# Router inputs as 32 long rows turned by the matrix engine, v loads moved ahead of later q and k, a third v buffer, routing constants on GpSimd, and a new order

## The chip, the cores and the metric

The kernel runs on one core of one Trainium2 chip. The metric is device time in microseconds of one launch. TensorE is called PE here, VectorE DVE, ScalarE ACT, GpSimd POOL and SyncE SP; PEld is PE's loading of weights, which the profile lists apart.

## What is computed

Chunked attention with 4 x 8 heads of 768 positions and 64 columns: each chunk of 32 queries sees 8 memory keys and up to 56 keys around it. Its output, 3072 tokens of 512 columns, goes through a router with noise, and each token through the best two of eight two-layer experts.

```python
def _attn_ref(q, k, v, mem_k, mem_v):            # q, k, v: (4, 8, 768, 64), mem_*: (4, 8, 8, 64)
    chunk, left_ctx, right_ctx = (32, 16, 8)
    for c in range(nc):
        k_full = np.concatenate([mem_k, k[:, :, l_start:r_end]], axis=2)
        v_full = np.concatenate([mem_v, v[:, :, l_start:r_end]], axis=2)
        scores = scale * np.matmul(q_c, k_full.transpose(0, 1, 3, 2))
        a = softmax(scores)
        out[:, :, c_start:c_end] = np.matmul(a, v_full)

def _moe_ref(x, w_gate, w_noise, noise, w1, w2): # x: (3072, 512), noise: (3072, 8), w_gate, w_noise: (512, 8)
    logits = x @ w_gate + np.log1p(np.exp(x @ w_noise)) * noise
    top2, top2_w = best two of the 8 logits, and their softmax
    for e in range(8):                           # w1: (8, 512, 1024), w2: (8, 1024, 512)
        for k in range(2):
            mask = top2[:, k] == e
            out[mask] += top2_w[mask, k, None] * (np.maximum(x[mask] @ w1[e], 0.0) @ w2[e])
```

## The kernel before

All work is recorded as operations with a label (`op("lq", ...)`), each with an engine or a choice of engines (`DA` means DVE or ACT), an assumed duration, the operations it depends on, the buffers it takes or uses, and a priority. A planner in Python runs through these once, before the program is built: on each engine it takes the operation that can start first, and among near ties the one of lowest priority number. The table `SHIFT` adds a number to the priority of every operation of a label. The instructions are then written in the order of the planned starts, so every engine executes a fixed row of instructions; what they really wait for is settled by semaphores at run time. POOL's row holds most DMA issues, SP's row the rest.

**Attention.** Sixteen pairs of heads, two pairs to a group. For each group POOL issues one load of q (`lq`, L468), one of k (`lk`), and two of v (`lv`, L479, two or three DMAs). v goes into a tile `vg` of which there are two (`NV`); a tile comes free when both pairs of its group have been through `pvo`. For each pair: `tq` and `tk` turn q and k on PE (L509), `eq` and `ek` copy them out of PSUM (DVE or ACT, L355 and L357 are the two engines' copy lines), `sc` makes the scores (L532, L539), `mx` and `sb` take the largest and subtract it on DVE (L546, L562), `ex` is the exponential on ACT (L565), `tp`/`ep` turn the result, `pvo` multiplies by v (L584, L587), `rc` and `ml` normalise on DVE (L592, L605), and `tx`/`exx` turn the 128 columns for the router. There is one score buffer `ps_s` and one output buffer `ps_o`.

**Routing.** After every four pairs one batch of 768 tokens is complete. Its router runs as `lg` (logits, PE), `r1` (ACT), then on DVE `r2` (L665 to L680, the choice of two), `r3s`, `r4`, `r7` (gates, L861 to L865), `r6` and `r8a` (place in a list, L727 to L744), `r8` (`ohv`, L702), with `r3` (ranks, L693) and `r9` (the table of row numbers, L751) on PE. Labels end in `_s` for the third batch and `_l` for the last. `row_write` (L871) puts the rows of a batch, with their gates, into the DRAM table `x_rows`. The router needs the noise `nz_all`, the weights `wgn` and constants (`c_small`, L396 to L415).

**Experts.** Tokens are grouped by the pair of experts they chose: 28 lists of 128. The first two experts are "sealed": half of each of their lists is filled from the first three batches, so POOL gathers those rows (L907) when the third router is done, PE turns them (L938, copied to `XS`), and the first layers of both (`fo_a`, L1013) run before the last batch is routed. The other half follows after the last router. Then second layers (`so`, L1054), scaling and adding on DVE (L1065, L1073), and a scatter of each finished list by POOL (L1085). Each gather but the first few of the last batch is followed by a filler `rest` (L910) on POOL. w1 has three buffers, w2 four, the gathered rows `xl` eight (`NXL`).

Of the kernel before, what the change touches and what calls it, by code (L numbers as in the profile page):

```python
# [24 lines left out]
    "c_ones": 54.3, "c_small": -12.1, "c_wg": -35.9, "c_wgl": 7.9, "eq": 52.4, "ex": 1.2, "fo_a": 31.9, "gather": 41.0, "gather_a": 21.0,  # L25
# [5 lines left out]
    "so": 22.7, "sscat": -0.4, "stab": 7.4, "stab_s": 0.6, "sum": -4.1, "t_mk": 15.4, "tab": -3.8, "tab2": 15.6, "tab_l": -11.6, "take_o":  # L31
    -1.7, "tq": -14.7, "tt": -28.0, "tt_a": -40.9, "w_row": -52.7, "xev": 8.3, "xev_a": -32.5, "yo": 8.0, "z_k": 24.3, "z_row": -41.4,
    "z_v": -3.3}
# [26 lines left out]
class Planner:  # L60


    def __init__(self):
        self.ops, self.slots, self.held = [], {}, {}
        self.late, self.made, self.taken = [], {}, {}
# [15 lines left out]
    def op(self, label, engs, fn, deps=(), alloc=(), use=(), prio=0.0, dma=None, tag="", pace=0.0, mm=0, after=()):  # L81
        if isinstance(engs, tuple):
            engs = [engs]
        o = Op(engs, fn, list(deps) + list(after), list(alloc), list(use), prio + SHIFT.get(label, 0.0), dma, tag)
        o.label = label
        o.pace, o.mm, o.after = pace, mm, set(after)
# [16 lines left out]
    def run(self):  # L103
        free, dma_free, sync_free, lanes, paced, products, busy = {}, 0.0, 0.0, [], 0.0, 0, 0.0
        ready = [o for o in self.ops if o.wait == 0]
        attn_left = sum(o.tag == "attn" for o in self.ops)
        attn_end = 0.0
        order = []
        while ready:
            cand = {}  # L110
            for o in ready:
# [12 lines left out]
                for eng, dur in o.engs:  # L124
                    est = max(free.get(eng, 0.0), at)
                    if o.pace and attn_left:
                        est = max(est, paced)
# [36 lines left out]
            else:  # L164
                o.done = o.end + 0.12
# [18 lines left out]
            if o.tag == "attn":  # L184
                attn_left -= 1
                attn_end = max(attn_end, o.done)
                if attn_left == 0:
                    for s in self.late:
                        s.at = attn_end
# [6 lines left out]
def kernel(  # L196
# [39 lines left out]
    NGE, NQ, NV = 2, 2, 2  # L236
    NXL, NXR, NW1, NW2, NACC = 8, 3, 1, 3, 20
# [44 lines left out]
    fill(pl.pool("w2", 1), early, [128, FB, Dm], BF16, "w2t")  # L282
# [36 lines left out]
    neg = const.tile([128, left_ctx], BF16, name="neg")  # L319
    ramp_i = const.tile([128, 128], I32, name="ramp_i")  # L320
# [14 lines left out]
    wgn_f = rp.tile([128, PB, 2, E], F32, name="wgn_f")  # L335
# [25 lines left out]

    def ident_fn(o):
        make_identity(nc, identb)

    c_ident = op("ident", ("POOL", 0.6), ident_fn, prio=-98.5)
    z_v = []
    for i, s in enumerate(v_slots):
        z_v.append([op("z_v", ("DVE", 1.35), lambda o, s=s, j=j: V.memset(s.tile[:, j], 0.0), prio=(-85 + 0.1 * j) if i == 0 else -60 + i + 0.1 * j) for j in range(2)])  # L368
    c_ident32 = op("c_ident32", ("DVE", 0.2), lambda o: (V.tensor_copy(ident, identb[:32, :32]), V.tensor_scalar(out=minus, in0=identb, scalar1=-1.0, scalar2=None, op0=Alu.mult)), deps=[c_ident], prio=-79)
    c_ones = op("c_ones", ("DVE", 0.1), lambda o: (V.memset(onesb, 1.0), V.memset(neg, NEG)), prio=-86)  # L370
# [24 lines left out]
    def small_fn(o):  # L395
        V.memset(smin, 0.0)  # L396
        V.memset(flip, 0.0)
        for p in flipped:
            V.memset(flip[:, col(*p):col(*p) + 1], float(SL))
        for e in range(NSEAL):  # L400
            for p in row_of(e):
                V.memset(smin[:, col(*p):col(*p) + 1], float(SL))
# [822 lines left out]
```

## Time and profile before

| | |
|---|---|
| median of 3 runs | 334.55 us (332.03 to 334.84) |
| the profiled execution | 331.19 us, of which the span of its instructions is 329.6 us |
| PE busy | 282.8 us, 86% of the span |
| DVE, ACT, POOL busy | 161.9, 141.0 and 127.4 us |
| bytes moved by DMA | 42.75 MB |

A row of a timeline reads: start, busy time, engine and line, operation, output from inputs, shapes, and in brackets how long the engine stood idle before it and what ended that. A row of stretches reads: from and to, length, busy time of PE, PEld, DVE, ACT and POOL with the instruction count, the clock that PE was granted, the busy share of the DMA engines (above 1 where transfers overlap) and GB/s written. Times within the profile count from the start of the span.

### The profile page before, as it was taken

How to read it: one execution, taken by the hardware profiler on the slowest of the kernel's cores; microseconds unless marked ns; L12 is line 12 of the kernel's file. 1: busy time of each engine (PE TensorE's matmuls, PEld its weight loads, DVE VectorE, ACT ScalarE, POOL GpSimd, SP SyncE). 2: the span in 40 equal slices, each digit the busy share in tenths (PEclk: the TensorE clock that was granted, in tenths of full speed). 3: DMA queues.
4: the chain of work that ended last, by engine and by line, in shares of the span. 5: the costliest groups of instructions: out<-in, count | busy, mean ns of one | idle time of the engine just before them, and what ended most of it. 6: DMA issues, size and time to landing. Idle time of an engine off the chain costs nothing.

```text
span 329.6 us, 7497 instructions
## 1 busy us (share of the span) xinstructions
PE 282.8 (86%) x3090; PEld 178.0 (54%) x3090; DVE 161.9 (49%) x404; ACT 141.0 (43%) x265; POOL 127.4 (39%) x148
## 2 busy tenths in 40 slices
PE   1678767587676799799999999999999999999991
PEld 0567655475566567455647645444544744744540
DVE  6877997879889676254253043052042051041050
ACT  1468665656484265741504604604604604505500
POOL 8293353413504915898735221041040051051072
PEclk9999797979785569999999999999999999999997
DMA  9999999999993592939999995395390020021032
GB/s 99 202 157 148 180 148 176 193 133 204 145 166 114 152 153 59 182 98 195 191 215 220 255 196 74 55 207 74 57 203 28 3 113 23 2 111 50 3 121 83
DMA packets 83065, 42.75 MB, mean 130 GB/s; under 512 B 57017, under 2 KB 76474, under 8 KB 83026
## 3 DMA queue, kind: packets, MB, share of 16 engines
q0 software_dynamic: 74672, 38.78, 87.3%
q1 hardware_dynamic: 8066, 3.38, 4.2%
q8 instruction: 25, 0.41, 0.5%
q14 instruction: 14, 0.11, 0.2%
q10 hardware_dynamic: 288, 0.07, 0.1%
HBM read 61.26 MB, written 10.85 MB: 219 GB/s over the span
## 4 chain that ended last, share of the span: by engine, by line
PE 50%; DMA 12%; POOL 12%; issue 11%; DVE 10%; ACT 2%; POOLq 1%; DVEq 0%
PE ps_l L1013 16%; PE ps_l L1054 15%; DMA vg<-in_v_dram 9%; PE ps_g L1054 6%; PE ps_g L1013 5%; POOL xl L907 4%; DMA w2l<-in_moe_w_dram 3%; POOL out_dram L1085 2%; POOL rest L910 2%; POOL vg L479 2%; DVE vg L368 2%; DVE xrow L605 2%; PE ps_o L587 1%; PE ps_g L614 1%; ACT kT L355 1%
## 5 line engine op out<-in xcount | busy, mean ns | idle before, releaser
L1023 ACT ACTIVATE ht<-ps_l 128x384 bf16<-128x384 f32 (+2 forms) x123 | 54.8, 470 | 94.5 <-PE ps_l L1013 93.0
L1054 PEld LDWEIGHTS <-ht 128*128 128x128 bf16 x448 | 43.7, 98 | 52.2 <-DMA w2l<-in_moe_w_dram 0.6
L1013 PE MATMUL ps_l<-XS,w1t 128*128 128x384 bf16 (+4 forms) x416 | 61.0, 302 | 2.8 <-ACT XS L355 2.8
L1013 PEld LDWEIGHTS <-w1t 128*128 128x128 bf16 x544 | 43.9, 99 | 33.4 <-issue 4.3
L1085 POOL DMA_INDIRECT out_dram<-acc,oid x28 | 28.8, 1027 | 70.2 <-DVE acc L1073 66.4
L1054 PE MATMUL ps_l<-w2l,ht 128*128 128x512 bf16 x240 | 53.4, 379 | 0.3 <-DMA w2l<-in_moe_w_dram 0.3
L479 POOL DMA_DIRECT2D vg<-in_v_dram x18 | 23.6, 1314 | 34.7 <-PE ps_o L587 30.6
L1073 DVE SCALAR_TENSOR_TENSOR acc<-ps_l,gates,acc 128x512 f32<-128x512 f32 x17 | 12.8, 751 | 45.6 <-PE ps_l L1054 43.6
L1073 DVE SCALAR_TENSOR_TENSOR acc<-ps_g,gates,acc 128x512 f32<-128x512 f32 x11 | 8.3, 751 | 37.4 <-PE ps_g L1054 37.4
L355 ACT COPY kT<-ps_q 64x768 bf16<-64x768 bf16 x27 | 21.4, 792 | 11.7 <-PE ps_q L509 10.2
L1065 DVE TENSOR_SCALAR acc<-ps_l,gates 128x512 f32<-128x512 f32 x20 | 15.0, 751 | 19.0 <-PE ps_l L1054 18.8
L1054 PE MATMUL ps_g<-w2l,ht 128*128 128x512 bf16 x96 | 21.7, 379 | 0.0
L907 POOL DMA_INDIRECT xl<-x_rows,gid x16 | 16.8, 1049 | 11.6 <-PE ps_l L1054 4.0
L1013 PEld LDWEIGHTS <-w1l 128*128 128x128 bf16 x192 | 17.2, 98 | 7.0
L1013 PE MATMUL ps_l<-XS,w1l 128*128 128x256 bf16 (+3 forms) x152 | 20.5, 289 | 0.0
L509 PE MATMUL ps_q<-identb,qn 128*64 128x128 bf16 x192 | 10.7, 256 | 10.8 <-DMA qn<-in_q_dram 7.3
L1023 ACT ACTIVATE ht<-ps_g 128x384 bf16<-128x384 f32 (+2 forms) x37 | 16.8, 479 | 6.7 <-PE ps_g L1013 5.8
L1013 PE MATMUL ps_g<-XS,w1t 128*128 128x384 bf16 (+4 forms) x128 | 19.6, 300 | 0.0
L919 DVE COPY gates<-xl 64x8 f32<-64x8 f32 (+1 forms) x40 | 11.5, 291 | 14.4 <-DMA xl<-x_rows,gid_b 8.3
L1054 PE MATMUL ps_l<-w2t,ht 128*128 128x512 bf16 x80 | 17.8, 379 | 0.0
L605 DVE TENSOR_TENSOR xrow<-ps_o,rec 128x384 bf16<-128x384 f32 x32 | 16.4, 553 | 0.5
L565 ACT ACTIVATE P<-sd 128x768 bf16<-128x768 f32 x16 | 13.5, 845 | 6.0 <-DVE sd L562 5.8
(170 smaller groups left out, 394.5 us busy)
## 6 DMA issues: line engine op xcount, KB each, us to landing
w1t<-in_moe_w_dram POOLq DMA_DIRECT2D x6, 1024.0 KB
w2l<-in_moe_w_dram POOLq DMA_DIRECT2D x6, 1024.0 KB
vg<-in_v_dram POOLq DMA_DIRECT2D x14, 336.0 KB
qn<-in_q_dram POOLq DMA_DIRECT2D x8, 384.0 KB
kn<-in_k_dram POOLq DMA_DIRECT2D x8, 384.0 KB
x_rows<-xrow SPq DMA_DIRECT2D x3, 792.0 KB, 9.0
w2t<-in_moe_w_dram POOLq DMA_DIRECT2D x2, 1024.0 KB
w1l<-in_moe_w_dram POOLq DMA_DIRECT2D x2, 1024.0 KB
```

Source lines behind the costliest of these rows:

```text
L355: A.copy(dst, src)
L479: G_.dma_start(out=vt.rearrange("p j c h d -> p (j c) h d")[p0 + j:p0 + j + nj, c:c + n, hh, :], in_=bass.AP(v.tensor, v.offset + (hd * S ...
L565: ex = op("ex", ("ACT", 0.85), lambda o, bsd=bsd, bP=bP: A.activation(out=bP.t.rearrange("p (x u) h c -> p x (u h) c", x=2), in_=bsd.t, fu ...
L605: V.tensor_tensor(out=x5[:, x], in0=ov(bO)[:, x, :, :, :D], in1=r5[:, x].to_broadcast([128, UB, 2, D]), op=Alu.mult)
L907: G_.indirect_dma_start(out=bx.t[:n], out_offset=None, in_=src, in_offset=bass.IndirectOffsetOnAxis(ap=ids_[:n, c:c + 1], axis=0), bounds_ ...
L919: V.tensor_copy(gates[rows, cc, :], bx.t[rows, XC:].bitcast(F32))
L1013: P_.matmul(out=dst, lhsT=w1b[e].t[:, kp, f * 128:(f + 1) * 128], rhs=src, start=(kp == 0), stop=(kp == KP - 1), skip_group_check=True)
L1023: A.activation(out=dst, in_=s_, func=Act.Relu)
L1054: P_.matmul(out=gy.t, lhsT=ht.t[:, f, j, :], rhs=w2b[e].t[:, f, :], start=(f == 0), stop=(f == FB - 1))
L1065: V.tensor_scalar(out=ba.t, in0=gy.t, scalar1=gate, scalar2=None, op0=Alu.mult)
L1073: V.scalar_tensor_tensor(out=ba.t, in0=gy.t, scalar=gate, in1=ba.t, op0=Alu.mult, op1=Alu.add)
L1085: G_.indirect_dma_start(out=out_part[nv], out_offset=bass.IndirectOffsetOnAxis(ap=oid[:, c:c + 1], axis=0), in_=ba.t, in_offset=None, boun ...
```

## The change

1. The noise (3072 x 8) and the two router weights (512 x 8) were loaded with 32 bytes to a piece. They are now read as 24 + 4 + 4 = 32 rows of 1024 numbers, into memory that `XS` uses later, turned by eight PE transposes (`t_wg`) and copied out by DVE (`c_wg`).
2. `vg` has three buffers. The first group's v, and `memv`, are loaded ahead of the second group's q and k. Clearing the v buffers may go to ACT (`clear`).
3. Most of `c_small` moves from DVE to POOL; four instructions stay on DVE as `c_smallv`. `r8` of the first three batches may go to POOL.
4. `ml` is one DVE instruction in place of two.
5. The third batch's row write is split, as the last one's was: the 512 columns as soon as its last `ml` is done, the gates after `r7`.
6. To make room, `xl` has six buffers and w2 three (all of them in memory that attention frees); w1 has four.
7. The planner: shorter durations for several PE operations, 0.3 us after PE in place of 0.12, a limit on PSUM buffers that ends with attention, and a `SHIFT` table that names single operations (`"fo#18"` is the nineteenth `fo`).

```diff
-    "c_ones": 54.3, "c_small": -12.1, "c_wg": -35.9, "c_wgl": 7.9, "eq": 52.4, "ex": 1.2, "fo_a": 31.9, "gather": 41.0, "gather_a": 21.0,
...
+    "c_mk": 31.9, "c_smallv": -11.9, "c_wg": 10.7, "ek#22": 43.7, "ek#9": 42.2, "ep": 98.8, "eq#6": -5.8, "ex": 191.7, "fo": 5.5, "fo#107":
...
-        if b.quota and self.held.get((b.cls, b.quota[0]), 0) >= b.quota[1]:
+        if b.quota and self.attn_left and self.held.get((b.cls, b.quota[0]), 0) >= b.quota[1]:
...
-                o.done = o.end + 0.12
+                o.done = o.end + (0.3 if eng == "PE" else 0.12)
...
-    NGE, NQ, NV = 2, 2, 2
-    NXL, NXR, NW1, NW2, NACC = 8, 3, 1, 3, 20
+    NGE, NQ, NV = 2, 2, 3
+    NXL, NXR, NW1, NW2, NACC = 6, 3, 2, 3, 20
...
-    fill(pl.pool("w2", 1), early, [128, FB, Dm], BF16, "w2t")
...
+    rows_f = XS[:32].bitcast(F32).rearrange("p a b c -> p (a b c)")[:, :128 * E]
...
+    def clear(eng, dst):
+        if eng == "ACT":
+            A.copy(dst, zero_b[:, :1].rearrange("p (a b c) -> p a b c", a=1, b=1).to_broadcast(list(dst.shape)))
+        else:
+            V.memset(dst, 0.0)
...
     def small_fn(o):
-        V.memset(smin, 0.0)
+        G_.memset(smin, 0.0)
...
-    c_small = op("c_small", ("DVE", 4.6), small_fn, deps=[c_pool, c_ident], prio=36)
+    c_small = op("c_small", ("POOL", 5.0), small_fn, deps=[c_pool], prio=36)
+    c_small_v = op("c_smallv", ("DVE", 0.8), small_v, deps=[c_pool], prio=36.5)
...
+        nc.sync.dma_start(out=rows_f[:NP], in_=moe_noise.rearrange("(t p) e -> t (p e)", p=128))
         for x, src in enumerate((moe_w_gate, moe_w_noise)):
-            nc.sync.dma_start(out=wgn_f[:, :, x, :], in_=src.rearrange("(kp p) e -> p kp e", p=128))
-        nc.sync.dma_start(out=nz_all, in_=moe_noise.rearrange("(t p) e -> p t e", p=128))
+            nc.sync.dma_start(out=rows_f[NP + PB * x:NP + PB * (x + 1)], in_=src.rearrange("(kp p) e -> kp (p e)", p=128))
...
+    def wg_turn(o):
+        for e in range(E):
+            P_.transpose(out=b_wg.t[:, 32 * e:32 * e + 32], in_=rows_f[:, e:128 * E:E], identity=ident)
...
+        V.tensor_copy(nz_all, g[:, :NP])
+        V.tensor_copy(wgn.rearrange("p k (x e) -> p x k e", x=2), g[:, NP:].rearrange("p (x k) e -> p x k e", x=2))
...
-    l_mv = op("l_mv", ("POOL", 6.0), memv_load, deps=[z_mv], prio=-97.2, dma=(0.5, 1.6))
...
+        if g == 0:
+            l_mv = op("l_mv", ("POOL", 3.4), memv_load, deps=[z_mv], after=lv[1:], prio=-96.5, dma=(0.5, 1.6))
...
-            for x in range(2):
-                V.tensor_tensor(out=x5[:, x], in0=ov(bO)[:, x, :, :, :D], in1=r5[:, x].to_broadcast([128, UB, 2, D]), op=Alu.mult)
+            V.tensor_tensor(out=x5, in0=ov(bO)[:, :, :, :, :D], in1=r5.to_broadcast([128, 2, UB, 2, D]), op=Alu.mult)
...
-            V.tensor_tensor(out=ohv, in0=R["pk"], in1=bt_n(tnum[:, BT * b:BT * (b + 1)]), op=Alu.mult)
+            (G_ if o.eng == "POOL" else V).tensor_tensor(out=ohv, in0=R["pk"], in1=bt_n(tnum[:, BT * b:BT * (b + 1)]), op=Alu.mult)
...
-        if b < B - 1:
+        if b < B - 2:
             rows_w[b] = [op("rows" + z, ("SP", 0.15), row_write, deps=[r7], use=[xr], prio=pr + 1, dma=(2.4, 1.8))]
...
-    QM = ("moe", 2)
+    QM = ("moe", 1)
```

What the new order makes of it is seen in three places. The numbers behind the names are buffer numbers of each build, and the line numbers are those of each kernel (the changed one's are 27 to 29 higher from attention on: its L495, L506, L478 are L468, L479, L452 of before).

**POOL at the start of the program.** Before, from its first load on:

```order
L468 DMA qn_95<-in_q_dram 128x4x384
...
L468 DMA kn_98<-in_k_dram 128x4x384
L468 DMA qn_96<-in_q_dram 128x4x384
L468 DMA kn_99<-in_k_dram 128x4x384
L468 DMA qn_97<-in_q_dram 128x4x384
L468 DMA kn_100<-in_k_dram 128x4x384
L452 DMA memv<-in_mem_v_dram 8x8x64 x4
L468 DMA qn_95<-in_q_dram 128x4x384
L479 DMA vg_101<-in_v_dram 40x64
L479 DMA vg_101<-in_v_dram 56x47x64
L468 DMA kn_98<-in_k_dram 128x4x384
L479 DMA vg_101<-in_v_dram 56x48x64
```

Now:

```order
L495 DMA kn_95<-in_k_dram 128x4x384
L495 DMA qn_92<-in_q_dram 128x4x384
L397 MEMSET upper 128x128
L398 AFFINE_SELECT upper<-upper 128x128
L399 IOTA ramp_i 128x128
L400 IOTA tok_i 128x24
L506 DMA vg_98<-in_v_dram 40x64
L506 DMA vg_98<-in_v_dram 56x47x64
L506 DMA vg_98<-in_v_dram 56x48x64
L478 DMA memv<-in_mem_v_dram 8x8x64 x4
L495 DMA qn_93<-in_q_dram 128x4x384
L495 DMA kn_96<-in_k_dram 128x4x384
```

Three groups' q and k, and a fourth q, stood ahead of the first v; one group's do now.

**DVE around the third batch's router.** `mx` and `sd` are the scores' largest value and the difference, `gid_s` the row numbers for the sealed gathers. Before, behind the router's `ohl`:

```order
L744 TENSOR_TENSOR ohl<-ramp,slot 128x768
L546 TENSOR_REDUCE mx_107<-ps_s_122 128x12
L765 SCALAR_TENSOR_TENSOR gid_s<-ps_g_88,tab 128x28
L760 SCALAR_TENSOR_TENSOR gid_s<-ps_g_88,tab 64x2x2
L760 SCALAR_TENSOR_TENSOR gid_s<-ps_g_88,tab 64x2
L778 TENSOR_TENSOR tab<-ps_g_88,tab 128x28
L562 TENSOR_TENSOR sd_109<-ps_s_122,mx_107 128x768
L592 RECIPROCAL rec_116<-ps_o_123 128x12
L605 TENSOR_TENSOR xrow_81<-ps_o_123,rec_116 128x3x2x64 x2
L736 SCALAR_TENSOR_TENSOR base_153<-ps_g_87,smin 128x28
L546 TENSOR_REDUCE mx_108<-ps_s_122 128x12
```

Now, at the head of the same router:

```order
L575 TENSOR_REDUCE mx_105<-ps_s_120 128x12
L591 TENSOR_TENSOR sd_107<-ps_s_120,mx_105 128x768
L621 RECIPROCAL rec_113<-ps_o_121 128x12
L633 TENSOR_TENSOR xrow_78<-ps_o_121,rec_113 128x6x2x64
L575 TENSOR_REDUCE mx_106<-ps_s_120 128x12
L591 TENSOR_TENSOR sd_108<-ps_s_120,mx_106 128x768
L693 TENSOR_TENSOR nn<-ns,nz_all 128x48
L694 TENSOR_TENSOR nl<-nn,ps_g_84 128x96
```

The last two pairs' `mx` and `sd` stood behind the third router on DVE; they now stand ahead of it.

**PE from the last router to the first expert.** `xl` are gathered rows of the sealed lists, `pk` and `ohl` come from the last router, `w1t_67` is the first expert's w1. Before, right behind the last router's logits:

```order
L938 LDWEIGHTS xl_74
L938 MATMUL ps_g_88<-identb,xl_74 128x128
...
L938 MATMUL ps_g_88<-identb,xl_75 128x64
L1013 LDWEIGHTS w1t_67
L1013 MATMUL ps_l_2456<-XS,w1t_67 128x384
...
L693 LDWEIGHTS upper
L693 MATMUL ps_l_2458<-pk,upper 128x168
```

Now:

```order
L966 MATMUL ps_g_84<-identb,xl_72 128x128
L721 LDWEIGHTS upper
L721 MATMUL ps_l_2432<-pk,upper 128x168
...
L966 MATMUL ps_l_2433<-identb,xl_74 128x64
L779 LDWEIGHTS ohl
L779 MATMUL ps_l_2434<-ohv,ohl 128x28
...
L1041 LDWEIGHTS w1t_67
L1041 MATMUL ps_l_2435<-XS,w1t_67 128x384
```

The first expert's first layer stood ahead of the last router's ranks and table on PE; it now stands behind both.

More of the change, by code (lines that the diff above doesn't have):

```diff
@@ L64, in __init__ @@
         self.ops, self.slots, self.held = [], {}, {}
-        self.late, self.made, self.taken = [], {}, {}
+        self.late, self.made, self.taken, self.seen = [], {}, {}, {}
     def pool(self, cls, n, late=False):
@@ L105, in run @@
         ready = [o for o in self.ops if o.wait == 0]
-        attn_left = sum(o.tag == "attn" for o in self.ops)
+        self.attn_left = sum(o.tag == "attn" for o in self.ops)
         attn_end = 0.0
@@ L125, in run @@
                     est = max(free.get(eng, 0.0), at)
-                    if o.pace and attn_left:
+                    if o.pace and self.attn_left:
                         est = max(est, paced)
@@ L319 @@
     neg = const.tile([128, left_ctx], BF16, name="neg")
+    zero_b = const.tile([128, 1], BF16, name="zero_b")
     ramp_i = const.tile([128, 128], I32, name="ramp_i")
@@ L683, in bt_n @@
             return ap.rearrange("p (t o) -> p t o", o=1).to_broadcast(n3)
-        r2 = op("r2" + z, ("DVE", 2.0), sel, deps=[r1, c_small], use=[gL], prio=pr)
+        r2 = op("r2" + z, ("DVE", 2.0), sel, deps=[r1, c_small, c_wg], use=[gL], prio=pr)
         gR = buf("G")
@@ L711 @@
         r3s = op("r3s" + z, ("DVE", 0.5), swap, deps=[r2, c_small], prio=pr + 0.03)
-        r8 = op("r8" + z, ("DVE", 0.25), hot_v, deps=[r2, c_small] + ([tabs[b - 1]] if b else []), prio=pr + 0.04)
+        r8 = op("r8" + z, [("DVE", 0.3), ("POOL", 0.6)] if b < B - 1 else ("DVE", 0.3), hot_v, deps=[r2, c_small_v] + ([tabs[b - 1]] if b else []), prio=pr + 0.04)
         def gate0(o, R=R, T=T):
```

81 lines of the change are left out of this document (42 added, 39 removed), and 16 rows, old and new, of the table SHIFT.

## Prediction

> **What bounds the kernel now.** I read the page's slices first, then two stretches of the span on either side of the first expert's first matmul (116.2 us).
>
> ```profile
> DVE  6877997879889676254253043052042051041050
> DMA  9999999999993592939999995395390020021032
> ```
> ```profile
> 0.00:115.71 115.71, 79.13 (x1778) 65.69 (x1779) 94.33 (x250) 63.88 (x91) 52.75 (x65) 0.86 1.60 158
> 116.20:322.30 206.10, 203.66 (x1312) 112.28 (x1311) 66.40 (x153) 76.64 (x174) 72.87 (x83) 0.99 0.57 115
> ```
>
> There are two programs in a row. From 116.2 to 322.3 PE is busy 203.66 of 206.1 us at a clock of 0.99: that part can hardly shrink, it can only start earlier. Before it, DVE is busy 94.33 of 115.71 us, PE only 79.13, and the DMA digits stand at 9 for twelve slices. So attention has two candidates, DVE and DMA, and DVE's waits say which one gives way where.
>
> ```profile
> DVE rec L592 <- PE ps_o L587: 5.1, 5, 1.6
> PE ps_o L587 <- DMA vg<-in_v_dram: 5.0, 3, 2.5
> POOL vg L479 <- PE ps_o L587: 30.6, 5, 7.8
> 35.04 15.57 DMA vg<-in_v_dram
> ```
>
> The chain of work that ended last runs through a v load for 15.57 us, issue to landing, and POOL stands 30.6 us in five waits for a v buffer. Yet the price of this is small: PE waits 5.0 us for v and DVE 5.1 us for PE. DVE works off what it has meanwhile. So attention is mostly DVE's own work with some 5 us of stalls by v.
>
> What would DMA alone need?
>
> ```profile
> 10.00:15.00 5.00, 3.38 (x74) 3.17 (x76) 3.77 (x12) 1.49 (x3) 1.94 (x3) 1.00 1.35 203
> 86.00:91.00 5.00, 3.95 (x56) 3.62 (x56) 4.06 (x12) 1.03 (x2) 1.89 (x2) 0.53 2.13 123
> 2.00:8.00 6.00, 0.73 (x12) 0.61 (x12) 4.80 (x8) 0.33 (x1) 5.92 (x11) 1.00 1.19 128
> vg<-in_v_dram POOLq DMA_DIRECT2D x14, 336.0 KB
> ```
>
> Where only q and k arrive, 203 GB/s are written, so a load of 384 KB takes 1.9 us; where only v arrives, 123 GB/s, so 336 KB takes 2.8 us. Sixteen of each make 76 us, one expert's w1 (1 MB, 5 us at 203 GB/s) comes between: an estimate of 85 us for the last v with the start-up. The last pairs' `ml` on DVE comes at about 100 us or later in any case I consider, so DMA doesn't set the end if POOL issues early enough. The noise's small pieces cost the opening at most 6 x (203 - 128) / 203 = 2.2 us of bandwidth. Since DVE is the tighter one, I count nothing for them; if I am wrong on that, 2.2 us is the gain, already inside the stalls' upper end below.
>
> **The change part by part.** I follow one instruction, `nn` of the last router (T), then the first expert's matmul behind it.
>
> Work that leaves DVE before T. First the constants:
>
> ```profile
> 24.43 0.08 DVE L396 MEMSET smin<- 128x28 f32 x1
> ...
> 25.27 0.15 DVE L403 TENSOR_SCALAR own<-tok_i 128x1 f32<-128x1 int32 x1 [0.38 <-POOL tok_i L389]
> ...
> 26.41 0.16 DVE L411 TENSOR_SCALAR upper_half<-tok_i 128x24 f32<-128x24 int32 x1
> 26.60 0.18 DVE L412 SCALAR_TENSOR_TENSOR tnum<-tok_i,upper_half 128x24 f16<-128x24 int32 x1
> ...
> 27.17 0.26 DVE L415 TENSOR_SCALAR ramp_s<-ramp_i 128x192 f16<-128x192 int32 x1
> 27.34 0.95 DVE L546 TENSOR_REDUCE mx<-ps_s 128x12 f32<-128x768 f32 x1
> ```
>
> From 24.43 to 27.34 is 2.9 us, of which 0.38 was a wait and the four that stay take 0.75: **1.8 us** go. POOL takes them on between its loads; its queue then has a backlog of DMA in front of it, which hides some microseconds there. Then the groups by shape:
>
> ```profile
> L605 DVE TENSOR_TENSOR xrow<-ps_o,rec 128x384 bf16<-128x384 f32 x32 | 16.4, 553 | 0.5
> L562 DVE TENSOR_TENSOR sd<-ps_s,mx 128x768 f32<-128x768 f32 x16 | 15.3, 954 | 0.5
> L357 DVE COPY kT<-ps_q 64x768 bf16<-64x768 bf16 x5 | 4.8, 955 | 2.2 <-ACT kT L355 2.2
> L357 DVE COPY xt<-ps_g 128x768 bf16<-128x768 bf16 x10 | 5.5, 554 | 1.6 <-PE ps_g L614 0.8 <-issue 0.5
> L702 DVE TENSOR_TENSOR ohv<-pk,tnum 128x168 f16<-128x168 bf16 x4 | 1.3, 327 | 0.0
> 110.67 1.02 DVE L605 TENSOR_TENSOR xrow<-ps_o,rec 128x384 bf16<-128x384 f32 x2
> ```
>
> In the new order DVE has one copy each of kT, qT and xt fewer (ACT takes them, and is busy only 63.88 us of this part): 0.95, as much for qT, which has as many columns, and 0.55, **2.5 us** together. Three `ohv` go to POOL: **1.0 us**. `ml` was two instructions in 1.02 us. One of 768 elements isn't in the trace: it lies between 0.954 us (the subtraction of the same size, also from PSUM) and twice 0.553; I take the former, for 16 pairs **1.1 us** (down to -1.4). Added is the copy of the noise (0.3, like `ramp_s`, which has as many elements). Sum: 1.8 + 2.5 + 1.0 + 1.1 - 0.3 = **6.1 us**. DVE's clearing of v buffers stays as it was: four memsets there, and ACT, which has nothing to copy before the first q and k land, clears the rest.
>
> The third buffer and the early v take away stalls of 0 to 5.1 us. A fixed order brings its own, which no row shows, so I take half, **2.5 us**. T moves from 115.71 to 115.7 - 8.6 = 107.1; the ends are 104.5 (all stalls go) and 113.9 (no stall goes, the constants bring nothing, `ml` loses).
>
> One row speaks against the move to POOL:
>
> ```profile
> 105.17 1.07 POOL L907 DMA_INDIRECT xl<-x_rows,gid_s  x1 [0.17 <-issue]
> 105.40 0.82 DVE L803 TENSOR_SCALAR cap<-cap 128x6 f32<-128x6 f32 x1
> ```
>
> The six elements of `cap` took 0.82 us and ended with POOL's gather, where the others took 0.17: POOL's work can hold DVE. At worst the constants then cost DVE as much as they free, and the 1.8 us drop out. The Trainium skill, "SBUF — State Buffer", section "SBUF: two separate sides", has a rule for it: DVE and GpSimd share one port pair as an exclusive lock, and DVE needs it in its two-port modes or with two SBUF inputs. By that rule the sum would lose less, since `mx`, `sd` and `ml` read PSUM.
>
> From T to the experts. Here the new order gives something back:
>
> ```profile
> 115.71 0.21 DVE L665 TENSOR_TENSOR nn<-ns,nz_all 128x48 f32<-128x48 f32 x1 [0.87 <-ACT ns L658]
> 118.74 0.20 DVE L861 TENSOR_TENSOR two<-key,m 128x48 f32<-128x48 f32 x1
> 120.18 0.33 DVE L727 TENSOR_TENSOR pos<-ps_l,pk 128x168 f32<-128x168 f32 x1 [0.21 <-PE ps_l L697]
> 120.98 0.17 DVE L802 TENSOR_REDUCE cap<-pk 128x6 f32<-128x24 bf16 x1
> 121.48 0.55 DVE L744 TENSOR_TENSOR ohl<-ramp,slot 128x768 f16<-128x768 f16 x1
> 116.20 3.14 PE L1013 MATMUL ps_l<-XS,w1t 128*128 128x384 bf16 x16 [0.73 <-ACT XS L355]
> 119.15 0.33 PE L693 MATMUL ps_l<-pk,upper 128*128 128x168 bf16 x1
> 119.93 0.88 PE L938 MATMUL ps_l<-identb,xl 128*128 128x128 bf16 x8
> 122.61 0.43 PE L751 MATMUL ps_l<-ohv,ohl 128*128 128x28 f16 x6
> 135.75 4.76 PE L1013 MATMUL ps_l<-XS,w1t 128*128 128x384 bf16 x48 [2.08 <-ACT XS L355]
> 163.25 1.90 PE L1054 MATMUL ps_l<-w2l,ht 128*128 128x512 bf16 x8 [0.33 <-DMA w2l<-in_moe_w_dram]
> ```
>
> The first expert's matmuls began 0.5 us after T; now the last router's table stands ahead of them on PE and waits for `ohl`. That ended 122.03 - 115.71 = 6.3 us after T; in the new order the gates (118.74 to 120.18) and `cap` (0.5) come behind it, which leaves 4.4. With 0.7 for the table and the signals the experts start at T + 5.1 = 112.2 in place of 116.2: **-4.0**. The ranks (119.15 to 119.93) and the table (0.3) no longer interrupt them: **-1.1**. The idle 2.08 us at 135.75 waited for the second halves' rows, whose gathers depend on T through the gate write, not on PE; they come earlier relative to PE now. I take half: **-1.0** (0 to -2.1). For fewer w2 and `xl` buffers I count 0: PE waited 0.33 us for w2 in the whole stretch, and in the new row on POOL the second w2 stands behind the same fourteen gathers; bounds 0 to +2. Sum **-6.1**.
>
> The profiled execution took 331.19 us, 1.6 more than its span and 3.4 less than the median of 334.55; the change is subtracted from the median: 334.55 - 6.1 = 328.45, say **328.4 us**.
>
> **The rivals.**
> *All stalls go.* T = 104.5, experts at 109.6: -6.6 - 1.1 - 2.1 = -9.8, 324.8 us. For it: the wait for `ps_o` is DVE's largest; against: only 5.0 us of PE's waits name v, and what DVE waits for PE and ACT otherwise doesn't hang on a v buffer.
> *The freed time turns into other waits.* One score buffer and one output buffer tie `mx`, `sd`, `ml` of successive pairs to PE and ACT, and the constants may be lost to the shared port. T = 111 to 114, experts at 116.1 to 119.1: -0.1 to +2.9, less 1.1 and up to 1.0 of idle time: -2 to +2, 332.5 to 336.5 us, no change. A change that doesn't do what it says ends here too: if the small pieces of noise never delayed a q or k that somebody waited for, and the third v buffer only moves a load from one wait to another.
> *Slower: the table ahead of the first expert.* PE cannot pass it. If T stays at 115.7, the experts start at 120.8: +4.6 - 1.1 = +3.5, 338 us, with up to 2 more if w2 comes late. The point from which this decides is T = 112.2: later than that, the change loses. It would take v loads held up behind POOL's new instructions (`ohv` waits for a router's choice, and loads queue behind it).
>
> **How the numbers follow.** Forecast (T 105.5 to 111) 0.55; all stalls go 0.17; other waits 0.18; slower 0.10. The likeliest gives 328.4. The runs of before spread from 332.0 to 334.8, so about 1.4 us go on both sides: 324.8 - 1.4, rounded to 323 below, and 336 above takes in the third case. About 1% (3.3 us) is what a measurement can tell from no change: faster than 331.2 us 0.68, within 0.24, slower 0.08 (part of the slow case is within 1%).
>
> **What would show it.** Right: the last `nn` near 107 us, DVE's wait for `ps_o` under 3 us up to there, the first expert's matmul some 5 us behind `nn`, PE full from it to its end in 203 to 206 us. Wrong: long waits of POOL at `ohv` with thin DMA digits behind, PE idle for w2 or `xl` after the start of the experts, or an `ml` above 1.02 us.

## The result, and the profile after

The changed kernel takes 336.36 us (median of 20 runs, 333.3 to 339.47), the kernel before 333.47 us (20 runs): ratio 1.006, 95% interval 1.0037 to 1.0083. It is slower by half a per cent; 328.4 us was forecast, with 323 to 336 as the range. The profiled execution took 335.80 us, with a span of 334.0; it is 4.6 us above the profiled one of before, which lay 2.3 us under its median.

The page's slices of DVE and DMA in the changed kernel, and the two stretches that were shown of before (up to the last `nn`; from the first expert's first matmul to PE's last):

```profile
DVE  6778858969888673342223036142022035032051
DMA  7999999999991574799999612978623620021022
```
```profile
0.00:115.04 115.04, 76.24 (x1778) 63.55 (x1778) 88.88 (x198) 70.09 (x93) 53.68 (x92) 0.86 1.70 157
120.18:326.60 206.42, 202.13 (x1285) 111.42 (x1300) 62.62 (x143) 75.88 (x169) 72.82 (x82) 0.99 0.56 114
```

DVE's work up to the last `nn` fell from 94.33 to 88.88 us, nearly as worked out. But `nn` came at 115.04 us, where 115.71 stood before: DVE's idle time rose from 21.4 to 26.2 us and ate the saving. Then the table stands ahead of the first expert, as the new order has it:

```profile
115.04 0.21 DVE L693 TENSOR_TENSOR nn<-ns,nz_all 128x48 f32<-128x48 f32 x1
119.27 0.56 DVE L772 TENSOR_TENSOR ohl<-ramp,slot 128x768 f16<-128x768 f16 x1
119.88 0.46 PE L779 MATMUL ps_l<-ohv,ohl 128*128 128x28 f16 x6 [0.97 <-DVE ohl L772]
120.18 3.15 PE L1041 MATMUL ps_l<-XS,w1t 128*128 128x384 bf16 x16
```

The first expert starts 5.14 us behind `nn`, at 120.18 in place of 116.20 us, and its stretch is as long as it was (206.4 and 206.1 us). So 4.0 of the 4.4 us between the spans of the two profiled executions are this start, and the question is why `nn` didn't come earlier. The waits up to `nn`, of DVE and of PE (total, times, longest), answer it; the last three rows are of the kernel before:

```profile
DVE mx L575 <- PE ps_s L571: 6.4, 5, 4.2
DVE rec L621 <- PE ps_o L616: 4.0, 7, 1.3
...
PE ps_s L568 <- issue: 4.9, 2, 4.0
PE ps_o L616 <- issue: 4.5, 3, 2.2
PE ps_q L538 <- issue: 2.9, 2, 2.2
PE ps_g L679 <- issue: 2.0, 1, 2.0
```
```profile
DVE mx L546 <- PE ps_s L542: 1.6, 3, 0.9
PE ps_q L509 <- issue: 3.2, 2, 2.1
PE ps_s L539 <- issue: 1.8, 1, 1.8
```

No wait of PE names v any more (5.0 us before). In its place PE stands 14.8 us at "issue" (5.8 us before), which is a wait for nothing that a semaphore shows. DVE sees it as waits for the scores: `mx` 6.4 us, where before had 1.6. The timeline of PE has the largest of these waits one by one (start, duration, line, and in brackets the idle time ahead); the last row is DVE's, behind the second of them:

```profile
36.78 0.23 PE L616 MATMUL ps_o<-vg,PT 128*32 128x128 bf16 x1 [1.85 <-issue]
45.16 0.28 PE L568 MATMUL ps_s<-kT,qT 128*32 128x112 bf16 x8 [3.96 <-issue]
52.73 0.74 PE L538 MATMUL ps_q<-identb,qn 128*64 128x128 bf16 x9 [2.18 <-issue]
60.08 0.27 PE L568 MATMUL ps_s<-kT,qT 128*32 128x112 bf16 x5 [0.92 <-issue]
72.75 0.63 PE L679 MATMUL ps_g<-wgn,xt 128*128 128x16 bf16 x18 [2.01 <-issue]
100.04 0.22 PE L616 MATMUL ps_o<-vg,PT 128*32 128x128 bf16 x1 [2.20 <-issue]
45.53 0.96 DVE L575 TENSOR_REDUCE mx<-ps_s 128x12 f32<-128x768 f32 x1 [4.17 <-PE ps_s L571]
```

They stand in the middle of a step (ahead of the last 8 of 24 score matmuls, of the last of 24 of `pv`), so no operand is late. DVE had nothing else to do at the second one and stood 4.17 us: this seventh of its sixteen `mx` came at 45.53 us, where the kernel before has 40.58, while the fourth had been level (27.42 and 27.34). Counted from 0 in the trace, weight loads included, the first instruction behind each wait is number 961, 1217, 1473, 1729, 2241, 3264 of PE's: multiples of 256 apart, the last one record short. The page's instruction queue moved 25 packets, and PE has some 6,200 instructions:

```profile
q8 instruction: 25, 0.41, 0.5%
```

0.41 MB in 25 packets are 16 KB each, 64 B for each of 256 instructions. In the trace every wait at such a number ends 1.4 to 1.8 us after such a packet has landed; for these six, packets ended at 34.99, 43.58, 51.09, 58.52, 71.25 and 98.52 us, PE going on at 36.78, 45.16, 52.73, 60.08, 72.75 and 100.04. **PE waits for its own code.** The Trainium skill, "Trainium Architecture — The Big Picture", section "The software stack", says that an instruction has 64 bytes, which agrees, and that the streams are copied to the engines when the program is loaded; this trace shows PE's arriving while it runs.

I call a block of 256 arrived 1.5 us after the end of its packet. So measured, a block arrives 6.2 to 8.3 us after PE has entered the one ahead of it, as long as attention loads. From number 705 to the wait that ends at 100.04 us are ten blocks; PE took 71.1 us for them (28.9 to 100.0), and 71.9 us before the change (30.5 to 102.4). In the kernel before, the same pace was there, half hidden: at the eight borders from 961 to 2753 PE either waited for code or came within 0.6 us of its arrival, since it had waited elsewhere.

### The profile page after: what moved, and what is told of

Read it like the earlier page. It is cut to its first block, busy times and chain, and to the rows that moved or that the text cites. A ratio compares the mean times of both kernels' runs of the same rounds, so it can differ in the third digit from the quotient of the medians.

```text
span 334.0 us, 7463 instructions
## 1 busy us (share of the span) xinstructions
PE 280.7 (84%) x3081; PEld 176.6 (53%) x3098; DVE 156.7 (47%) x358; ACT 148.1 (44%) x267; POOL 132.4 (40%) x180
## 4 chain that ended last, share of the span: by engine, by line
PE 54%; issue 12%; DMA 11%; POOL 9%; DVE 8%; ACT 2%; POOLq 1%; DVEq 0%
PE ps_l L1041 17%; PE ps_l L1082 16%; PE ps_g L1082 5%; DMA qn<-in_q_dram 5%; PE ps_g L1041 5%; DMA w2l<-in_moe_w_dram 4%; POOL xl L935 3%; DMA kn<-in_k_dram 3%; PE ps_q L538 2%; POOL vg L506 2%; PE ps_o L616 2%; POOL out_dram L1113 2%; PE ps_o L613 2%; DVE xrow L633 2%; POOL rest L938 2%
## 5 line engine op out<-in xcount | busy, mean ns | idle before, releaser
L1051 ACT ACTIVATE ht<-ps_l 128x384 bf16<-128x384 f32 (+2 forms) x113 | 49.3, 465 | 66.5 <-PE ps_l L1041 65.6
L1082 PE MATMUL ps_l<-w2l,ht 128*128 128x512 bf16 x326 | 74.8, 379 | 0.5
L1041 PEld LDWEIGHTS <-w1t 128*128 128x128 bf16 x416 | 31.2, 99 | 20.5 <-issue 1.6
L1041 PE MATMUL ps_l<-XS,w1t 128*128 128x384 bf16 (+4 forms) x312 | 40.5, 287 | 1.0 <-ACT XS L360 1.0
L1041 PE MATMUL ps_l<-XS,w1l 128*128 128x384 bf16 (+3 forms) x247 | 40.5, 316 | 0.1
L1041 PEld LDWEIGHTS <-w1l 128*128 128x128 bf16 x320 | 30.0, 98 | 18.6
L506 POOL DMA_DIRECT2D vg<-in_v_dram x18 | 23.7, 1326 | 13.7 <-PE ps_o L616 7.9
L1093 DVE TENSOR_SCALAR acc<-ps_l,gates 128x512 f32<-128x512 f32 x14 | 10.5, 751 | 24.1 <-PE ps_l L1082 17.6
L575 DVE TENSOR_REDUCE mx<-ps_s 128x12 f32<-128x768 f32 x16 | 15.2, 953 | 6.4 <-PE ps_s L571 6.4
L360 ACT COPY qT<-ps_q 128x768 bf16<-128x768 bf16 x15 | 12.0, 798 | 11.7 <-PE ps_s L571 5.4
L633 DVE TENSOR_TENSOR xrow<-ps_o,rec 128x768 bf16<-128x768 f32 x16 | 15.3, 956 | 0.5
```

The lines of the kernel that those rows point to most:

```text
L360: A.copy(dst, src)
L506: G_.dma_start(out=vt.rearrange("p j c h d -> p (j c) h d")[p0 + j:p0 + j + nj, c:c + n, hh, :], in_=bass.AP(v.tensor, v.offset + (hd * S ...
L575: mx = op("mx", ("DVE", 0.98), lambda o, bmx=bmx, bS=bS: V.tensor_reduce(out=bmx.t, in_=sv(bS), axis=AX, op=Alu.max), deps=[sc], alloc=[bm ...
L633: V.tensor_tensor(out=x5, in0=ov(bO)[:, :, :, :, :D], in1=r5.to_broadcast([128, 2, UB, 2, D]), op=Alu.mult)
L1041: P_.matmul(out=dst, lhsT=w1b[e].t[:, kp, f * 128:(f + 1) * 128], rhs=src, start=(kp == 0), stop=(kp == KP - 1), skip_group_check=True)
L1051: A.activation(out=dst, in_=s_, func=Act.Relu)
```

## The experiments

Here is what the profiled execution of each showed; "code" are PE's waits at "issue" ahead of the last `nn`, "v" those for v, "DVE" DVE's busy time up to it. The ratio is to the kernel before, of the timed runs.

```
kernel           ratio (95%)              nn      code    v   DVE    first expert
before           1                       115.71    5.8  5.0  94.33   116.20
after            1.006  (1.0037-1.0083)  115.04   14.8  0.0  88.88   120.18
half_after       334.42 us, no interval  111.59    0.3  5.0  88.47   116.76
half_before      1.0029 (0.999-1.0067)   114.07    2.6  7.6  95.01   115.42
pad2_after       1.0093 (1.0041-1.0145)  114.26   11.2  0.0  89.03   119.41
nov_after        0.9846 (0.981-0.9882)   110.49    6.2  0.0  88.39   115.62
nov_half_after   0.9743 (0.9671-0.9816)  106.27    0.6  0.0  88.66   111.41
both_before      0.9851 (0.98-0.9903)    112.49    0.0  4.4  94.45   113.37
mlsplit_after    1.0039 (1.0006-1.0072)  114.47   12.0  0.0  89.41   119.61
both_mlsplit     0.984  (0.9787-0.9893)  107.41    2.0  0.7  88.77   112.55
mlone_before     0.9986 (0.9955-1.0016)  116.58    3.3  9.1  92.65   117.07
nv2b_after       1.011  (1.0052-1.0169)  114.28    7.9  3.1  88.25   119.41
tab_late         1.0044 (1.0008-1.0081)  112.98   12.2  0.0  89.16   114.94
tab_late2        1.0025 (0.9991-1.006)   113.86   12.0  0.0  89.05   115.82
tab_late3        1.0284 (1.0237-1.0331)  113.99   11.4  0.0  88.21   116.98
tab_late4        1.0016 (0.9979-1.0052)  116.65   12.5  0.0  88.53   118.15
rows_before      1.0047 (1.001-1.0084)   117.46    1.5  6.0  94.11   118.04
```

One caution for reading it: after and the four runs named tab_late have the same attention, and their last `nn` lies between 112.98 and 116.65 us. So a difference of `nn` below some 4 us between two single executions shows little; the sums of waits differ by more. All variants with half, pad, nov or both in their names, and nv2_after, compute something else than the reference; they are there for their time alone.

**Fewer PE instructions.** In half_after the turns of q and k are halved:

```
+            f = src.t.rearrange("p h e -> p (h e)")
             for t in range(TP):
-                for hh in range(2):
-                    P_.transpose(out=dst.t[64 * hh:64 * hh + 64, t * QP:(t + 1) * QP], in_=s[:, j + 2 * hh, t, :], identity=identb)
+                P_.transpose(out=dst.t[:, t * QP:(t + 1) * QP], in_=f[:, 384 * j + 64 * t:384 * j + 64 * t + 128], identity=identb)
```

> The changed kernel with half of the turns of q and k left out: one 128-column transpose where two of 64 columns stood, so 24 PE instructions fewer for each of the 16 pairs (384 in all; its q and k are not the right ones). Everything else stays in its place, DVE's work too. Theory A (PE waits for its own code: a block of 256 instructions every 6.2 to 8.4 us between 29 and 100 us): one and a half blocks fewer, the last router's nn 5 to 9 us earlier than 115.0 as far as DVE can follow, 328 to 332 us. Theory B (DVE's work and the order behind the third router set the end of attention, code waits fall into time that DVE doesn't miss): nn within 1.5 us, 335 to 337.5 us.

The code waits went, all but 0.3 us, and `nn` came 3.4 us earlier, at 111.59 us, less than the 5 to 9 us of theory A. What took their place is in PE's waits:

```profile
PE ps_o L616 <- DMA vg<-in_v_dram: 5.0, 4, 3.0
```

PE reached v before v was there, as in the kernel before. The time was 334.42 us (median of 10 runs, 327.57 to 336.81, too wide apart for an interval), between the two theories, so the totals don't decide here.

The filled variants put one small matmul ahead of each remaining transpose, so that the count is the changed kernel's again:

```
 pad_after   +   P_.transpose(out=dst.t[:32, t * QP:t * QP + 32], in_=identb[:32, :32], identity=identb[:32, :32])
 pad2_after  +   P_.matmul(out=dst.t.bitcast(F32)[:, 64 * t:64 * t + 1], lhsT=identb, rhs=identb[:, :1], start=True, stop=True)
```

> The same with a transpose of 32 x 32 of the identity ahead of each transpose of q and k: the same number of PE instructions as the changed kernel, with less work in them (same values left out as in the run with half of the turns). Theory A (it is the number of instructions that counts): code waits come back, nn at 115 within 1.5 us, 335 to 338 us. Theory C (it was PE's work in the turns that counted): as with half of the turns, 328 to 332 us. Theory B: 335 to 337.5 us, but then the run with half of the turns is there too.

This one failed as a test: 370.7 us. PE was busy in 74.79 of the 75 us from 25 to 100 us; a filler and the transpose behind it took 0.35 us together:

```profile
32.12 0.20 PE L538 MATMUL ps_q<-identb 32*32 32x32 bf16 x1
32.26 0.29 PE L539 MATMUL ps_q<-identb,kn 128*128 128x128 bf16 x1
32.48 0.20 PE L538 MATMUL ps_q<-identb 32*32 32x32 bf16 x1
32.61 0.29 PE L539 MATMUL ps_q<-identb,kn 128*128 128x128 bf16 x1
```

> The changed kernel with half of the turns left out, and a full-size matmul of one column ahead of each of the others: the number of PE instructions of the changed kernel, with little work in the added ones. (An earlier filling with 32 x 32 transposes drained PE at each change of size.) Theory A (the number counts): code waits of PE in attention of 8 us or more, nn at 113.5 to 116 us. Theory C (PE's work counts): nn at 111 to 112.5 us, as with half of the turns alone.

With full-size fillers the code waits were back at 11.2 us, the largest again at 961, 1217, 1473 and 2241, and ratio 1.0093 is the changed kernel's or worse. It is the number of instructions that brings the waits, not the work in them. (`nn`, 2.7 us behind half_after, agrees but couldn't show it alone.)

> The kernel before with half of the turns of q and k left out in the same way (384 PE instructions fewer, its q and k are not the right ones). Theory A, that attention went at the pace of PE's code before the change too (ten blocks took 71.9 us there from 30.5 to 102.4 us, 71.1 us in the changed kernel): 3 to 7 us faster than before, 326 to 330.5 us. Theory B' (as predicted: the kernel before went at the pace of DVE's work with stalls by v): within 1.5 us of before, 332 to 335 us.

In the kernel before the same cut did nothing to the time. Code waits fell to 2.6 us and waits for v rose to 7.6: theory A as I had put it, with PE's code as the pace of that kernel, is refuted. Code is one of its limits, and v stands right behind it.

**Fewer v packets.** nov_after returns from `v_load` at once for groups 3 to 7 (`if g >= NV: return`).

> The changed kernel with the v loads of the fourth and later groups left out (10 of 16 loads; the old v is used again). PE's instructions and all else stay. No wait of PE in the changed kernel names v, so if v counts it is through the queues. Theory A2 (the code blocks wait behind v's small packets): a block comes in about 6 us in place of 7.1, code waits fall from 14.8 to under 7 us, nn 3 to 8 us earlier, 328 to 333 us. Theory A1 (a block's time doesn't depend on v): code waits stay above 11 us, nn within 1.5 us, 335 to 337.5 us.

It is 1.5% faster than before, and 2% faster than the changed kernel, though no wait of PE had named v. Nearly all that is left of code waits ends by 45.2 us; v's last packets land at 42.0 us:

```profile
PE ps_s L570 <- issue: 4.3, 1, 4.3
PE ps_o L618 <- issue: 1.8, 1, 1.8
```

Behind that a block arrives 3.4 to 6.1 us after the border ahead of it, against 6.2 to 8.3 us: PE's code comes sooner without v's loads. That is theory A2 as far as v delays the code. Whether the size, the number or the bytes of v's packets do it isn't separated; and the edit also took work from POOL (39.0 us busy up to `nn`, 53.7 in the changed kernel), so not all of the gain need be code.

**Both at once.**

> Both reliefs at once in the changed kernel: the v loads of the fourth and later groups left out and half of the turns of q and k left out. With v left out alone nn came at 110.5 us, with half of the turns alone at 111.6 us, where waits for v came back (5.0 us). Theory A (PE's code and v's packets take each other's place, and DVE is the next bound): code waits under 5 us in all, no wait for v, nn at 106 to 109 us. Theory E (the end of attention has its own chain, one score and one output buffer and the third router's work on DVE in between): nn at 110 to 111.5 us in spite of both.

> The kernel before with both reliefs (half of the turns of q and k and the v loads of the fourth and later groups left out), as it was done with the changed kernel, where the last nn came at 106.3 us with 88.7 us of DVE's work ahead of it. Theory A (three limits lie close together in both kernels: DVE's work, PE's code, v; with the two others away DVE's 5.5 us of difference show at full price): nn at 111 to 113 us, 5 to 6.5 us behind the changed kernel with both reliefs. Theory G (the changed order or its buffers cost something of their own that these reliefs hide): nn at 106 to 109.5 us, as in the changed kernel.

(Here the test is `g >= NV + 1`, with `NV` of 2, so that the same groups are left out.)

```profile
106.27 0.21 DVE L695 TENSOR_TENSOR nn<-ns,nz_all 128x48 f32<-128x48 f32 x1 [0.49 <-ACT ns L688]
0.00:106.27 106.27, 73.36 (x1586) 61.98 (x1586) 88.66 (x199) 69.85 (x93) 39.21 (x82) 0.87 1.10 138
```
```profile
112.49 0.21 DVE L667 TENSOR_TENSOR nn<-ns,nz_all 128x48 f32<-128x48 f32 x1 [0.60 <-ACT ns L660]
0.00:112.49 112.49, 76.54 (x1586) 65.95 (x1586) 94.45 (x250) 63.59 (x90) 38.61 (x54) 0.86 1.04 131
```

The first pair of rows is the changed kernel, the second the kernel before, each with both reliefs. DVE's idle time is the same in both, 17.6 and 18.0 us, and `nn` differs by 6.2 us where DVE's work differs by 5.8. With code out of the way and most of v, the saving counts at full price. One thing is not equal: in the old order PE still waits 4.4 us for v, 3.9 of it at 51.5 us, and in the new one not at all; that this cost DVE nothing is read from the two sums of idle time. That `nn` lies near the 107.1 us of the prediction is luck, for it takes reliefs that the prediction didn't have. Theory A held in both, E and G fell. The times, 326.0 and 329.06 us, differ by less, since the changed kernel gives back 4.3 us behind `nn` (start of the experts at +5.14 against +0.88 us).

**More or less of DVE's work.** mlsplit_after takes the multiplication apart into its two halves again, mlone_before puts it into one instruction in the old kernel.

> The changed kernel with the multiplication by the reciprocal in two instructions again (1.11 us in place of 0.956 for each of 16 pairs, 2.4 us more of DVE's work ahead of the last nn). Theory A (DVE isn't what attention waits for; its savings of 5.5 us went into waits for PE): within 1 us of the changed kernel, 335 to 337.5 us. Theory B (DVE's work counts at full price, as predicted): 2 us or more on top, 338 to 340 us.

> The kernel before with one part of the change alone, the multiplication in one instruction (0.956 in place of 1.11 us, 16 times: 2.4 us less of DVE's work, where 1.1 was predicted by the row of 1.02). Theory A (in the kernel before DVE's saved work is lost to PE's code and v as well): within 1 us of before, ratio 0.997 to 1.003. Theory B' (as predicted: DVE's saved work comes off the end of attention at full price): 2 to 2.5 us faster, ratio 0.993 or less.

> The changed kernel with both reliefs and the multiplication in two instructions again, 2.4 us more of DVE's work. In the changed kernel itself this edit moved nothing (nn 114.5 after 115.0 us). Theory A (DVE is the bound once code and v are out of the way): nn at 108 to 109.5 us in place of 106.3, 328 to 329.5 us in place of 326.0. Theory E (a chain at the end of attention holds, not DVE): nn within 0.8 us of 106.3.

The dose was smaller than I had written: two halves overlap, and DVE's busy time rose by 0.5 us in mlsplit_after (89.41 after 88.88) and fell by 1.7 in mlone_before. So mlsplit_after, the same as the changed kernel within the intervals, decides little. In mlone_before 1.7 us of DVE's work brought 0.5 us (interval -1.5 to +0.5), and the waits for v rose to 9.1 us: less than the full price, as theory A has it. In both_mlsplit `nn` moved by 1.1 us and the time by 2.0, the way of theory A, but with DVE's busy time up by 0.1 us only; it stays inconclusive.

**Two parts alone.** nv2_after gave the v groups two buffers in turn, without moving the loads:

> The changed kernel with two v buffers in place of three (groups take buffers 0 and 1 in turn; the third lies idle), everything else in its place. Theory A (attention goes at the pace of PE's code, the third buffer only takes away waits that would lie beside it): nn at 115 to 117 us, code waits of PE go down by about what waits for v come back (2 to 5 us), 335.5 to 338.5 us. Theory V (the third buffer carries a real gain that something else eats): nn at 118 us or later, 339 us or more.

It was no test: loads now overtook the readings of the group that had their buffer, so the kernel computed something else, and its 376.7 us say nothing of the third buffer. nv2b_after moves each load behind these readings.

```
+    pvs = [o for o in sorted(order, key=lambda o: pl.ops.index(o)) if o.label == "pvo"]
+    for g in range(NG):
+        groups[g][2].slot = v_slots[g % 2]
+        for l in groups[g][5] if g > 1 else []:
+            x = max(order.index(p) for p in pvs[2 * g - 4:2 * g - 2])
+            if order.index(l) < x:
+                order.remove(l)
+                order.insert(x, l)
```

> The changed kernel with two v buffers in place of three, now with each v load put behind the last reading of the group that had its buffer (in the earlier attempt loads overtook the readings, so that it computed something else). Theory A (attention goes at the pace of PE's code, the third buffer takes away waits that lie beside it): waits of PE for v return (3 to 8 us), code waits fall by about as much, nn at 114 to 117 us, 335 to 338.5 us. Theory V (the third buffer carries a real gain): nn at 118 us or later, 339 us or more.

Waits for v came back (3.1 us) and code waits went down (7.9 us), with `nn` where it was. The third buffer turns waits of one kind into the other; of 1.011 against 1.006 the intervals overlap.

> The kernel before with one part of the change alone: noise and router weights read as 32 long rows, turned by PE (8 transposes) and copied by DVE behind the copy of the memory keys. Predicted for this part: nothing, at most 2.2 us of gain if its 32 B packets held up a q or k that somebody waited for; 0.3 us of DVE's work come on top. Theory A (DVE's work and PE's code set the pace, the opening waits are hidden): within 1 us of before, 332.5 to 335 us. Theory D (small packets hold the opening): 1.5 to 2.5 us faster.

rows_before puts the 32 long rows and their 8 transposes into the kernel before. It was 0.5% slower, 1.0047 (1.001 to 1.0084): neither theory. The opening shows where it starts:

```profile
12.45 1.08 PE L448 MATMUL ps_g<-ident,XS 32*128 32x32 f32 x8 [2.85 <-DVE mkT L445]
17.01 0.96 DVE L552 TENSOR_REDUCE mx<-ps_s 128x12 f32<-128x768 f32 x1 [0.86 <-PE ps_s L548]
```

The edit put the transposes behind the copies of the memory keys and ahead of the first k on PE, where they stood 2.85 us for these copies; the first `mx` came 2.8 us later than before (14.23 us), and `nn` 1.75 us. So this run can't tell the rows from their place, and its profiled execution was the longest of its ten (337.97 us). In the changed kernel the same transposes run at 7.02 us, ahead of the first q; its first `mx` is late too, at 16.35 us, but its fourth is level again.

**The order behind the last router.** tab_late puts the first expert's first two groups ahead of the ranks:

```
+    ahead_of(by["r3_l"][0], [by["tt_a"][1]] + by["xev_a"][2:4] + by["fo_a"][:2])
+    ahead_of(by["r6_l"][0], [by["r5_l"][0], by["r7_l"][0]])
```

> The changed kernel with the old order at one place: the second transposes of the sealed rows and the first two matmul groups of the first expert stand ahead of the last router's ranks and table on PE, and the gates ahead of the positions on DVE. All else, attention too, stays. Theory A (4 us of the loss lie in this order, since the last nn came at 115.0 and the first expert had to wait 5.1 us behind it): first expert's matmul at 116.5 to 117.5 us in place of 120.2, the ranks interrupt again (+1.1), sum -2 to -3: 333 to 334.5 us. Theory B (what comes forward waits elsewhere, at the gathers behind the gate rows): within 1 us of the changed kernel, 335.5 to 337.5 us.

The first expert started 1.96 us behind `nn` in place of 5.14, but PE then stood 1.6 us for the table and 1.0 us for the spare ranks. tab_late2 moves these behind further groups (`ahead_of(r9_l, [tt_a#2, fo_a#2, tt_a#3])`, `ahead_of(s1_l, [fo_a#3])`, `ahead_of(s3_l, [fo_a#4])`):

> The run with the old order at one place (first expert ahead of the last router's ranks) goes on here: the table comes behind the third matmul group and the second sealed transposes, the spare ranks behind the fourth. In that run PE stood 1.6 us for the table and 1.0 us for the spare ranks inside the first expert, which ate half of what the earlier start gave. Theory A (those 2.6 us are what is left): the two waits go, 1.5 to 2.5 us less than there, ratio to before 0.994 to 1.0. Theory B (later ids delay the second halves' gathers, PE waits for rows instead): ratio as there, 1.003 to 1.006.

```profile
115.82 3.15 PE L1041 MATMUL ps_l<-XS,w1t 128*128 128x384 bf16 x16 [0.90 <-ACT XS L360]
123.08 0.93 PE L1041 MATMUL ps_l<-XS,w1t 128*128 128x384 bf16 x8 [1.00 <-DVE gid L793]
164.96 1.90 PE L1082 MATMUL ps_g<-w2l,ht 128*128 128x512 bf16 x7 [1.55 <-DMA w2l<-in_moe_w_dram]
```

The start came 4.4 us earlier than in the changed kernel (1.2 of it by an earlier `nn`), and the ratio went from 1.006 to 1.0025, 1.2 us, with intervals that overlap. Ranks (0.8 us) and table (0.4) stand inside the experts again, and PE waits for a result of DVE and for w2.

> The run with the first expert's groups ahead of ranks and table, and on POOL the second weight matrix of the first expert behind four of the second halves' gathers (it shared the queues with the write of the gate rows that these gathers wait for) and that of the second expert four gathers earlier (PE waited 1.5 us for it). Theory A (both waits go): gathers 2 to 3 us earlier, PE's idle time in the experts 5.6 to about 3 us, ratio to before 0.990 to 0.997. Theory B (the gate rows' write takes its time without the weights too, or the weights come late instead): ratio 0.999 to 1.005.

> The run with the first expert's groups ahead of ranks and table (1.0025 of before), with one more edit on POOL: the second expert's second weight matrix is loaded four gathers earlier, while the first expert's stays where it was (moved behind gathers it had made later gathers wait, 5.1 us of PE's time). Theory A (the wait of PE for that matrix, 1.5 us, goes and nothing takes its place): ratio 0.995 to 1.000. Theory B (the gathers behind the load come late in their turn): ratio 1.002 to 1.010.

tab_late3 lost: 1.0284 (1.0237 to 1.0331). The second halves' gathers did start earlier (124.18 us, 127.60 in tab_late2), but the ones behind them then stood behind the moved matrix:

```profile
148.19 1.03 PE L966 MATMUL ps_l<-identb,xl 128*128 128x128 bf16 x8 [5.08 <-DMA xl<-x_rows,gid_b]
```

tab_late4, with the second expert's matrix alone moved, took PE's wait for it away and is as fast as the kernel before, 1.0016 (0.9979 to 1.0052), between its two theories. No version that computes the right thing was faster than the kernel before beyond its interval.

## Why the prediction was wrong, step by step

- **What bounds attention: this step failed.** "So attention is mostly DVE's own work with some 5 us of stalls by v" left out PE's code. The rows with "issue" stood in the waits of the kernel before (3.2 and 1.8 us), and I read past them. The sum moved T by the whole of DVE's saving and half of v's stalls, 8.6 us; it moved by 0.7, since PE's waits for code grew from 5.8 to 14.8 us. Three limits lie within a few us of each other: DVE's work, v, and the arrival of PE's code beside v's packets. Taking one away shows the next.
- **DVE's work, -6.1 us:** right, -5.45; `ml` took 956 ns, 954 were forecast. By the rule of the shared port (the Trainium skill, "SBUF — State Buffer", section "SBUF: two separate sides") the constants on POOL might have blocked DVE; in the total no more shows of it than the 0.65 us by which the saving fell short.
- **Stalls by v, -2.5 us of DVE's time:** wrong. PE's waits for v went whole (5.0 to 0), but DVE's idle time rose by 4.8 us, and a single wait behind late code is 4.17 us. The rival of the freed time turning into other waits named this kind of outcome (with T at 111 to 114, where 115.04 came), and score and output buffers as the place; it was code.
- **The last v at 85 us:** in the trace v's packets end at about 95 us. It wasn't what held the end, but by nov_after it held the code.
- **T + 5.1:** right, 5.14, by two misses that cancel: `ohl` ended at T + 4.8 in place of 4.4, and 0.35 us followed in place of 0.7.
- **Ranks no longer interrupt, -1.1:** right in kind, PE's busy time in the experts fell by 1.5 us. **Idle of the second halves, -1.0:** wrong, the idle time in that stretch rose from 2.4 to 4.3 us, 1.0 of it for w2, which was counted at 0 within 0 to +2.
- **The slower rival** had the mechanism behind T, the point (T later than 112.2) and about the price: its sum gives +2.8 us for T = 115.04, and the medians differ by +2.9, the profiled executions by +4.6. Its chance was 0.10. Its cause was not the one named: POOL did wait 24.0 us for a router's choice at `ohv`, but no wait of PE for v followed, and the DMA digits stay at 9 up to 100 us.

Of the chances 0.72 went to cases in which DVE's idle time shrinks. But even with both reliefs 17.6 us of it are left: most of DVE's idle time was never v's to give back.

## What to carry to other kernels

Where PE runs many small matmuls, count its instructions: waits at "issue" that stand multiples of 256 instructions apart were code that had not arrived here, and they shrank when other loads were left out. Before a saving on the busiest engine is put at full price, ask of each other resource how long it would need alone for the same stretch; here DVE's saving of 5.5 us moved the end of attention by 0.7 us, and a saving of 5.8 us by 6.2 once code and v were relieved in both kernels. And an order that moves work ahead of the next stage's start is paid in full as soon as the gain in front of it fails to come.

## What the hardware showed

- PE's code came in packets of 16 KB, 256 instructions, during the run. A block arrived 6.2 to 8.3 us after the border ahead of it beside v's 128 B packets, 3.4 to 6.1 us without them; where PE stood waiting, it went on 1.4 to 1.8 us after the packet's end.
- A 32x32 transpose between full-size ones made a pair of the two take 0.35 us (32.12 to 32.48 us above). The Trainium skill, "TensorEngine Tiling (Array Packing)", section "Key Properties", says that a change of the tiling mode drains TensorE; the rows show the time, not the drain itself. The full-size fillers of pad2_after, as many, added 3.1 us to PE's busy time up to `nn` (78.55 and 75.47 us).
